# Output projection on two column groups of 256 outputs, in place of four of 128

## The chip, the cores and the metric

The kernel runs on one core of a Trainium2 chip. Of its engines, TensorE runs the matmuls and writes their sums into a memory called PSUM, VectorE and ScalarE copy results out of PSUM, and SyncE issues the transfers (DMA). A column group is a set of 32 of the columns of TensorE's array, which hold the 32 output rows here; groups can work side by side. The metric is the device time of one execution in microseconds (us), so lower is better. Profiles are of one execution; their span, from the first to the last instruction, is about 1.8 us shorter than the time.

## The reference

One decode step of attention with grouped heads: 32 sequences, one query row each, 32 query heads over 8 key/value heads of 128 values, a window of the last 512 of 2048 cached rows, and an output projection `wo` from 4096 to 512.

```
W = min(4096, max(256, Sk // 4))                    # 512
q = (x @ wq) as heads [32, 32, 1, 128]
k, v = the last W rows of k_cache, v_cache, each kv head repeated 4 times
scores = einsum("bhqd,bhkd->bhqk", q, k) * 128 ** -0.5
p = softmax(scores)
o = einsum("bhqk,bhkd->bhqd", p, v)
return o.reshape(32, 1, 4096) @ wo                  # the part that is changed
```

All inputs and the output are bfloat16. The output is 32 rows of 512 values.

## The kernel before

One queue (SyncE's) loads everything but the small input `x`: `wq`, then the blocks of K and V in a fixed order, then `wo` as eight head groups of 512 rows. The last group's load is cut in two: rows 0 to 2 of the four that each partition holds, and then row 3 alone. The kernel starts the output projection when the last V block has been used and the attention output has been brought into the order that it needs (`o_sel`). The parts that matter, with cuts marked:

```python
WO_CUT = 3
out_sb = x_sb.rearrange("b (c n) -> b c n", c=4)
# SyncE ...
for hg in range(NHG):                                      # 8 head groups
    for i0, i1 in ((0, 4),) if hg < NHG - 1 else ((0, WO_CUT), (WO_CUT, 4)):
        sp.dma_start(wo_sb[:, hg, i0:i1]..., wo[hg * 512:(hg + 1) * 512, :]...
        ).then_inc(sem_last if i0 else sem_wo[hg], 16)
sp.wait_ge(dve_out, 2)
sp.wait_ge(act_out, 2)
sp.dma_start(out..., out_sb...).then_inc(sem_out, 16)
# TensorE ...
for hg in range(NHG):
    pe.wait_ge(sem_wo[hg], 16)
    for i in range(4):
        if hg == NHG - 1 and i == WO_CUT:
            pe.wait_ge(sem_last, 16)
        for c in range(4):                                 # four column groups of the array
            ins = pe.matmul(
                X_ps[32 * c:32 * (c + 1), 2, 0:128],
                lhsT=o_sel[:, i, hg, :],
                rhs=wo_sb[:, hg, i, c * 128:(c + 1) * 128],
                start=(hg == 0 and i == 0), stop=(hg == NHG - 1 and i == 3),
                tile_position=(0, 32 * c),
            )
ins.then_inc(pe_fin, 1)
# VectorE, after pe_fin; ScalarE does the same with c = 2, 3
for c in range(2):
    dve.tensor_copy(out_sb[:, c, :], X_ps[32 * c:32 * (c + 1), 2, 0:128]).then_inc(dve_out, 1)
```

## Time and profile before

| | before |
|---|---|
| median time, 6 runs | 187.70 us (187.51 to 188.07) |
| span of the profiled execution | 185.9 us |
| the projection on TensorE | 128 matmuls, 178.72 to 183.27 us |
| start of the last head group to the end of the last copy | 182.71 to 183.91: 1.20 us |
| issue of the store | 183.98 us |

The prediction below shows the lines of the page and of the end of the timeline. Read them so: the DMA row says that the transfers fill the span, and the timeline says what still runs while the last of them land and after that. The row "start of the last head group to the end of the last copy" is the yardstick in the whole text: it does not depend on when the stream of transfers ends.

### The profile page before, as it was taken

To read this page: it belongs to the slowest core of one execution; us is meant where nothing else is said; L and a number is where in the kernel's file an instruction comes from. 1 tells how busy PE (TensorE), PEld (TensorE's weight loads), DVE (VectorE), ACT (ScalarE), POOL (GpSimd) and SP (SyncE) were. 2 spreads that over 40 slices of the span, in tenths; PEclk is the share of its full clock that TensorE was granted. 3 is DMA by queue.
4 is the path that set the end of the run, shared out by engine and by line. 5 is a ranking of instruction groups with operands and counts; after the bars stand their busy time and mean duration, and the time that the engine had idled before them with its cause. 6 is when DMAs were issued, how large, how long until landed. Compare 5 with 4: busy or idle time off the path is not lost.

```text
span 185.9 us, 3842 instructions
## 1 busy us (share of the span) xinstructions
PE 109.0 (59%) x1604; PEld 89.4 (48%) x1604; DVE 131.9 (71%) x239; ACT 82.3 (44%) x142; POOL 32.0 (17%) x82
## 2 busy tenths in 40 slices
PE   0232004336179906929906994159979975998752
PEld 0100001022069805819606974019949975987741
DVE  0006999689999999993699987999999995010001
ACT  3001000269320397020695018925998999910011
POOL 7100390500700080060240041000040000000000
PEclk9999999955557985885985599576999999999998
DMA  6999999999999999999999999999999999999980
GB/s 194 434 448 412 437 423 423 448 412 437 420 416 441 416 427 434 416 437 427 423 421 423 441 423 420 434 423 430 428 412 434 427 423 430 420 423 411 405 332 27
DMA packets 6304, 75.80 MB, mean 408 GB/s; under 512 B 720, under 2 KB 912, under 8 KB 1936
## 3 DMA queue, kind: packets, MB, share of 16 engines
q1 hardware_dynamic: 6240, 75.53, 96.4%
q8 instruction: 12, 0.20, 0.4%
q10 hardware_dynamic: 48, 0.03, 0.1%
q14 instruction: 4, 0.03, 0.0%
HBM read 75.53 MB, written 0.03 MB: 406 GB/s over the span
## 4 chain that ended last, share of the span: by engine, by line
DMA 64%; DVE 20%; PE 9%; issue 3%; SPq 3%; DVEq 0%
DMA V_sb<-in_v_cache_dram 31%; DMA K_sb<-in_k_cache_dram 14%; DMA w_sb<-in_wo_dram 12%; DVE KT_sb L431 12%; PE O_ps L356 8%; DMA w_sb<-in_wq_dram 6%; DVE w_sb L453 4%; DVE QA_sb L421 2%; SPq L214 2%; PE X_ps L299 1%; SPq L202 1%; DVE oT_sb L414 0%; DVE KT_sb L409 0%; PE X_ps L393 0%; DVE maxv L438 0%
## 5 line engine op out<-in xcount | busy, mean ns | idle before, releaser
L431 DVE STREAM_TRANSPOSE KT_sb<-K_sb 128x2048 uint32<-128x2048 uint32 x32 | 72.3, 2287 | 1.3 <-DMA K_sb<-in_k_cache_dram 1.1
L356 PE MATMUL O_ps<-w_sb,V_sb 128*128 128x128 bf16 x640 | 47.0, 244 | 9.6 <-DVE w_sb L453 5.0
L356 PEld LDWEIGHTS O_ps<-w_sb,V_sb 128*128 128x128 bf16 x640 | 45.6, 110 | 12.3 <-DVE w_sb L453 6.5
L268 POOL COPY QBD<-QA_sb 32x64 bf16<-32x64 bf16 x64 | 25.6, 540 | 81.2 <-PE S_ps L319 63.6
L520 ACT ACTIVATE w_sb<-PTc,mask 128x512 bf16<-128x512 bf16 x60 | 38.9, 729 | 0.0
L319 PE MATMUL S_ps<-KT_sb,QBD 128*32 128x512 bf16 x256 | 20.7, 475 | 26.6 <-DVE KT_sb L431 20.2
L453 DVE TENSOR_SCALAR w_sb<-PTc,mask 128x512 bf16<-128x512 bf16 x100 | 30.2, 370 | 6.3 <-PE O_ps L356 6.3
L319 PEld LDWEIGHTS S_ps<-KT_sb,QBD 128*32 128x32 bf16 x256 | 7.5, 110 | 36.5 <-issue 32.4
L492 ACT ACTIVATE X_ps<-S_ps,negmax 128x512 f32<-128x512 f32 x8 | 5.3, 657 | 42.8 <-DVE negmax L440 42.8
L338 PE MATMUL PT_ps<-P_bf,pick 128*128 128x128 bf16 x128 | 11.4, 260 | 17.9 <-ACT P_bf L501 14.7
L338 PEld LDWEIGHTS PT_ps<-P_bf,pick 128*128 128x128 bf16 x128 | 9.8, 119 | 20.9 <-ACT P_bf L501 16.3
L530 ACT ACTIVATE oT_sb<-O_ps 128x128 bf16<-128x128 f32 x8 | 6.0, 750 | 28.2 <-PE O_ps L356 28.2
L356 PE MATMUL O_ps<-K_sb,V_sb 128*128 128x128 bf16 x256 | 14.9, 217 | 3.5 <-DMA V_sb<-in_v_cache_dram 2.2
L356 PEld LDWEIGHTS O_ps<-K_sb,V_sb 128*128 128x128 bf16 x256 | 14.5, 96 | 4.3 <-issue 2.5
L520 ACT ACTIVATE K_sb<-PTc,mask 128x512 bf16<-128x512 bf16 x24 | 15.3, 725 | 1.6 <-DVE KT_sb L431 1.6
L453 DVE TENSOR_SCALAR K_sb<-PTc,mask 128x512 bf16<-128x512 bf16 x40 | 12.1, 377 | 0.3 <-ACT PTc L511 0.2
L474 DVE CAST K_sb<-S_ps 128x256 bf16<-128x256 f32 x1 | 0.4, 425 | 14.3 <-PE S_ps L368 14.3
L356 PE MATMUL O_ps<-KT_sb,V_sb 128*128 128x128 bf16 x128 | 7.5, 217 | 2.3 <-DMA V_sb<-in_v_cache_dram 2.3
L356 PEld LDWEIGHTS O_ps<-KT_sb,V_sb 128*128 128x128 bf16 x128 | 7.3, 96 | 2.5 <-issue 2.5
L520 ACT ACTIVATE KT_sb<-PTc,mask 128x512 bf16<-128x512 bf16 x12 | 7.7, 728 | 0.0
L501 ACT ACTIVATE P_bf<-X_ps,recip 128x512 bf16<-128x512 f32 x8 | 5.5, 684 | 4.5 <-DVE recip L446 4.4
L409 DVE CAST KT_sb<-X_ps 128x512 bf16<-128x512 f32 x1 | 0.7, 692 | 9.2 <-PE X_ps L299 9.2
(41 smaller groups left out, 49.6 us busy)
## 6 DMA issues: line engine op xcount, KB each, us to landing
K_sb<-in_k_cache_dram SPq DMA_DIRECT2D x16, 2048.0 KB, 15.1
V_sb<-in_v_cache_dram SPq DMA_DIRECT2D x16, 2048.0 KB, 16.8
w_sb<-in_wq_dram SPq DMA_DIRECT2D x2, 2048.0 KB, 9.7
w_sb<-in_wo_dram SPq DMA_DIRECT2D x7, 512.0 KB, 19.8
w_sb<-in_wo_dram SPq DMA_DIRECT2D x1, 384.0 KB, 22.6
w_sb<-in_wo_dram SPq DMA_DIRECT2D x1, 128.0 KB, 14.4
oT_sb<-in_x_dram ACTq DMA_DIRECT2D x1, 32.0 KB, 4.4
out_dram<-oT_sb SPq DMA_DIRECT2D x1, 32.0 KB, 1.5
```

Of the source, the lines that this page charges most:

```text
L214: sp.dma_start(wo_sb[:, hg, i0:i1].rearrange("p i n -> p (i n)"), wo[hg * 512:(hg + 1) * 512, :].rearrange("(m i) n -> m (i n)", i=4)[:, i ...
L268: pool.tensor_copy(dst[:, i, :, x0:x0 + 4], src).then_inc(pool_qbd, 1)
L319: ins = pe.matmul(S_ps[32 * c:32 * c + 32, q % 2, :], lhsT=QBD[:, q % 2, g, b, e, :], rhs=bass.AP(tensor=KT_sb, offset=s0 * slot + (b * G ...
L338: ins = pe.matmul(PT_ps[:, r, :], lhsT=pick[:, r, KS - s:KS - s + P], rhs=P_bf[:, s, :], start=(s == 0), stop=(s == KS - 1), tile_position ...
L356: ins = pe.matmul(O_ps[:, q % 2, 0:P], lhsT=V_sb[:, m % NV, r, :], rhs=z_of(q)[:, :, x0 + r, :], start=(e == 0 and r == 0), stop=(e == 1 a ...
L421: dve.tensor_copy(QA[32 * a:32 * a + 32, c], QW[32 * c:32 * c + 32, :, :, a::4].rearrange("p h k q -> p h q k"),).then_inc(dve_q, 1)
L431: dve.transpose(KT_w[:, n % NK, b].rearrange("p i r s -> p r i s"), K_w[:, n % NK, :, 32 * b:32 * b + 32],).then_inc(dve_T, 1)
L453: ins = dve.tensor_scalar(z_of(q)[:, k].rearrange("p x r -> p (x r)"), PTc[:, q % RING].rearrange("p x r -> p (x r)"), mask[:, k:k + 1], N ...
L492: act.activation(P_f32, S_ps[:, q % 2, :], ACTF.Exp, bias=negmax[:, q:q + 1], scale=SCALE, accum_out=sums[:, q:q + 1],).then_inc(act_exp, 1)
L501: act.activation(P_bf[:, :, :], P_f32.rearrange("p (x s) -> p s x", s=KS), ACTF.Copy, scale=recip[:, q:q + 1],).then_inc(act_P, 1)
L520: ins = act.activation(z_of(q)[:, k].rearrange("p x r -> p (x r)"), PTc[:, q % RING].rearrange("p x r -> p (x r)"), ACTF.Copy, scale=mask[ ...
L530: act.activation(oT_sb[:, :, 4 * q:4 * q + 4].rearrange("p h a -> p a h"), O_ps[:, q % 2, 0:P].rearrange("p (a h) -> p a h", a=4), ACTF.Co ...
```

## The change

Its intent is to have fewer and larger instructions at the end: half as many matmuls, and one copy for each engine in place of two. The words that came with it also name the load of one `wo` row for each partition at the end, which the diff does not touch. The diff, whole but for its line numbers and context:

```diff
-        out_sb = x_sb.rearrange("b (c n) -> b c n", c=4)
+        out_sb = x_sb.rearrange("b (c n) -> b c n", c=2)
...
-            sp.wait_ge(dve_out, 2)
-            sp.wait_ge(act_out, 2)
+            sp.wait_ge(dve_out, 1)
+            sp.wait_ge(act_out, 1)
...
-                    for c in range(4):
+                    for c in range(2):
                         ins = pe.matmul(
-                            X_ps[32 * c:32 * (c + 1), 2, 0:128],
+                            X_ps[32 * c:32 * (c + 1), 2, 0:256],
                             lhsT=o_sel[:, i, hg, :],
-                            rhs=wo_sb[:, hg, i, c * 128:(c + 1) * 128],
+                            rhs=wo_sb[:, hg, i, c * 256:(c + 1) * 256],
...
-            for c in range(2):
-                dve.tensor_copy(
-                    out_sb[:, c, :], X_ps[32 * c:32 * (c + 1), 2, 0:128]
-                ).then_inc(dve_out, 1)
+            dve.tensor_copy(out_sb[:, 0, :], X_ps[0:32, 2, 0:256]).then_inc(dve_out, 1)
...
-            for c in range(2, 4):
-                act.activation(
-                    out_sb[:, c, :], X_ps[32 * c:32 * (c + 1), 2, 0:128], ACTF.Copy
-                ).then_inc(act_out, 1)
+            act.activation(out_sb[:, 1, :], X_ps[32:64, 2, 0:256], ACTF.Copy).then_inc(act_out, 1)
```

## The prediction

> **What bounds the kernel now.** I read the page first, for the engine shares, the slices and the chain that ended last. The lines that carry it:
>
> ```profile
> PE 109.0 (59%) x1604; PEld 89.4 (48%) x1604; DVE 131.9 (71%) x239; ACT 82.3 (44%) x142; POOL 32.0 (17%) x82
> DMA  6999999999999999999999999999999999999980
> HBM read 75.53 MB, written 0.03 MB: 406 GB/s over the span
> DMA 64%; DVE 20%; PE 9%; issue 3%; SPq 3%; DVEq 0%
> ```
>
> No engine is near full, but the row of the 16 DMA engines is at 9 tenths from the second slice to the last but one. The kernel streams 75.53 MB, and the chain of waits is mostly transfers (64%). The change touches no transfer (the order of the SyncE instructions is the same in both kernels), so only the last slice and a half can move: what still runs once the stream is ending. For that I read the order of time of the last microseconds (start us, us, engine, line, operation, count, idle before it and what released it):
>
> ```profile
> 178.72 1.30 PE L393 MATMUL X_ps<-w_sb,K_sb 128*32 128x128 bf16 x80 [0.52 <-DVE K_sb L474]
> 180.52 0.41 PE L393 MATMUL X_ps<-w_sb,K_sb 128*32 128x128 bf16 x16 [0.50 <-DMA w_sb<-in_wo_dram]
> 181.75 0.41 PE L393 MATMUL X_ps<-w_sb,K_sb 128*32 128x128 bf16 x16 [0.82 <-DMA w_sb<-in_wo_dram]
> 182.71 0.56 PE L393 MATMUL X_ps<-w_sb,K_sb 128*32 128x128 bf16 x16 [0.55 <-DMA w_sb<-in_wo_dram]
> 183.32 0.56 ACT L547 ACTIVATE oT_sb<-X_ps 32x128 bf16<-32x128 f32 x2 [5.81 <-PE X_ps L393]
> 183.32 0.59 DVE L477 CAST oT_sb<-X_ps 32x128 bf16<-32x128 f32 x2 [4.66 <-PE X_ps L393]
> 183.98 0.36 SPq L220 DMA_DIRECT2D out_dram<-oT_sb  x1
> ```
>
> These are the output projection: eight head groups of 16 matmuls, one per wo block. The first five blocks are there when it starts at 178.72; groups 5, 6 and 7 each wait for their block, so by then TensorE follows the DMA. Cut more finely, the last 16 split in two: 12 start by 182.9, the other four at 183.03, which is where the separate last 128 KB load (issued about 168.5, 14.4 us to landing, so about 182.9) lets them go. They end at 183.27, two copies run on VectorE beside two on ScalarE, and the last copy ends at 183.32 + 0.59 = 183.91. Then the store is issued at 183.98 and the span ends at 185.9. **The path of the tail:** landing of the last wo row, last matmuls, evacuation, store.
>
> The words of the change name a last load of one wo row for each partition. The kernel before has that load already (its cut is at row 3 of 4) and the diff does not touch it. I give it no gain.
>
> **What the Trainium skill says.** (1) "TensorE: Matmul & The Clock Gate", section "Single matmul latency": a warm matmul of N columns takes (398+N)/2.4 ns. For N = 128 that is 219 ns; this trace has 219 as the median of the projection's 128 matmuls, and a granted clock of 1.00 from 176 to 184 us, so it agrees. The same formula gives 272.5 ns for N = 256. (2) "TensorEngine Tiling (Array Packing)", section "Tiling Modes": with 128 rows and 32 columns there are four tiles, which work independently. The trace agrees: 80 matmuls in 1.30 us are (1.30 - 0.219)/79 = 13.7 ns from start to start, a quarter of the 53.3 ns that 128 columns take at 2.4 GHz. (3) "ScalarE: Activation LUTs", section "What ACT_TABLE_LOAD costs": an activation with immediate scale and bias takes 186 ns + 0.833 ns per element, which is 293, 506 and 612 ns at 128, 384 and 512; the trace has 270, 490 and 597, so the slope agrees and the constant is some 20 ns lower here. (4) "DMA: Bandwidth & Descriptors", section "Where the ~2 µs actually goes": most of a small transfer's fixed time is the receipt of the write. The store of 32 KB took 1.5 us from issue to landing here, and its size and shape in memory stay, so I leave it alone.
>
> **The change part by part.**
>
> Matmuls: 128 of 128 columns on four column groups become 64 of 256 columns on two. The streamed columns stay 16,384, but half as many groups take them at once. A pair of 256 columns occupies its groups for 256/2.4 = 107 ns, so the whole projection needs 32 x 107 = 3.4 us of streaming in place of 128 x 13.7 = 1.75 us. Fewer instructions is therefore more TensorE time. Where does it lie?
> - Groups 0 to 4: 20 rounds, the last of which starts at 178.72 + 19 x 0.107 = 180.75 and ends at 181.02, in place of 180.02.
> - Group 5's block was there at 180.52 at the latest, so it follows at once: four rounds, 180.86 to 181.18, ending near 181.45 in place of 180.93.
> - Group 6's block comes at 181.75. The array has been free since about 181.3, so the lag is gone with 0.4 us to spare. It runs to 181.75 + 3 x 0.107 + 0.27 = 182.34.
> - Group 7 starts at 182.71 as before. Three rounds for its first three rows start at 182.71, 182.82 and 182.92; the array is free for the fourth at 183.03, which is just when the last load releases it. So the last pair starts at 183.03 as before, or a few tens of ns later, and ends one longer latency on: + (272.5 - 219) = +0.05 us. Before, the last of four starts some ten ns after the first; that is now one pair. Net **+0.04 us** on the path.
>
> Evacuation: two copies of 32x128 on each engine become one of 32x256. VectorE from PSUM in this trace: 280 ns for 128 elements per partition, 425 for 256 (the 128x256 copy of the last selection), 556 for 384, 692 for 512, or about 1.06 ns per element on 145 fixed. I take 0.42 us for 32x256, since the time follows the elements per partition. It was 0.59 with the gap between the two: -0.17. ScalarE: 270 for 128, 490 for 384, so about 0.38 for 256 in place of 0.56: -0.18. VectorE remains the later one, so **-0.17 us** on the path.
>
> Store, waits and the rest: the SyncE waits count 1 instead of 2 on each engine; no cost. The 32 rows of 1 KB in the output tile are the same bytes. 64 matmuls and 64 weight loads fewer are less to fetch, but TensorE does not bound the place where they are. **0.**
>
> Sum: +0.04 - 0.17 = -0.13 us. In the trace's terms the last copy ends at 183.32 + 0.04 + 0.42 = 183.78 and not 183.91, so the time becomes 187.71 - 0.13 = 187.58, which I call **187.6 us**.
>
> **The rivals.**
>
> TensorE becomes the bound of the tail. If the two groups did not overlap (64 x 107 = 6.8 us), or if the clock were granted at half (32 rounds of 213 ns, the same 6.8 us), the projection would end at 178.72 + 6.8 + 0.2 = 185.7 rather than 183.27, so the time would be some 2.4 us longer, 190.0 us (+1.3%), still within 2%. Against it: the four groups overlap fully before, and the clock reads 1.00 throughout that stretch. The change keeps TensorE busier there, so the clock should not fall. I give this 4%.
>
> A smaller form: only the last block sees it. If group 7's first six matmuls are not through when the last row lands (a landing earlier than 183.03 with the same landing of the 384 KB), the fourth round waits for the third and up to 0.1 us of the copy's gain is given back: 187.65 to 187.7. The spare is nil by my working, so I give that one chance in three.
>
> The evacuation's gain is hidden. It would be if the store waited for something else. But the page of the DMA queue's own waits shows the store waiting 13.4 us with ScalarE's copies named as the releaser, and it is issued 0.07 us after the last copy. There is no other wait between. Yet 0.13 us is 0.07% of the time, and the three runs before lie between 187.68 and 188.07, so the gain can drown in the jitter of a stream of 75 MB: 187.7 to 187.9 measured, with the mechanism right.
>
> The stream itself changes. It would take another order of transfers or another time at which a buffer comes free; the first 178 us of every engine's program are the same in both kernels, so I see no path to it.
>
> **Range and chances.** 187.58 is the centre of the sum. Below, I allow 0.3 us: the gain is at most the whole 0.17 of the copies plus jitter of the stream. Above, 0.4: the before-runs reach 0.36 above their median. So 187.3 to 188.0 should hold it 8 times in 10. A change of 2% would be 3.75 us. The whole of the tail after the last landing is about 3 us and the worst case of TensorE is +2.4, so neither side is within reach by this mechanism: faster 0.01, same 0.98, slower 0.01.
>
> **What would show it right or wrong.** In the profile of the changed kernel the projection should be 64 matmuls of about 272 ns, the first 40 lasting about 2.3 us instead of 1.30; group 6 and 7 should still be released by a wo transfer; the last pair should end within 0.1 us of the old distance from the last landing; one copy of about 0.42 us on VectorE and 0.38 us on ScalarE should stand before the store, which should again follow within 0.1 us; and the span should be near 185.8. It is wrong if TensorE is still busy with an earlier group when group 6's or 7's block lands (no idle ahead of the group), if the 32x256 copy costs as much as the two did, or if the transfers land at other times than before for a reason outside the change.

## More of the kernel before

The 32 output rows of a column group land on their own 32 partitions of PSUM, so the four groups' results lie on four sets of 32 partitions, and the copies bring them side by side onto the partitions 0 to 31 for the store.

## The result

The changed kernel took 187.60 us (median of 6 runs, 187.29 to 188.04) against 187.70 us of the kernel before. The ratio is 0.9992 with a 95% interval of 0.9976 to 1.0007: the same within noise. Ratios here are worked out from the fast runs of both kernels, and not quite the ratio of the medians quoted.

The page of the changed kernel, same rows as in the prediction:

```profile
PE 109.5 (59%) x1540; PEld 90.0 (48%) x1540; DVE 131.5 (71%) x238; ACT 82.3 (44%) x141; POOL 32.0 (17%) x82
DMA  6999999999999999999999999999999999999980
HBM read 75.53 MB, written 0.03 MB: 407 GB/s over the span
DMA 56%; DVE 26%; PE 11%; issue 4%; SPq 3%; DVEq 0%
```

There are 64 matmuls fewer (1604 to 1540) and yet TensorE is busy a little longer. The DMA row is the same digit for digit. The shares of the chain differ in its earlier part, in which none of the changed lines stands; why was not followed up. The end of the timeline of the changed kernel (start us, us, engine, line, operation, count, idle before and its releaser):

```profile
178.67 2.80 PE L393 MATMUL X_ps<-w_sb,K_sb 128*32 128x256 bf16 x48 [0.52 <-DVE K_sb L474]
181.83 0.61 PE L393 MATMUL X_ps<-w_sb,K_sb 128*32 128x256 bf16 x8 [0.36 <-DMA w_sb<-in_wo_dram]
182.80 0.61 PE L393 MATMUL X_ps<-w_sb,K_sb 128*32 128x256 bf16 x8 [0.35 <-DMA w_sb<-in_wo_dram]
183.45 0.37 ACT L543 ACTIVATE oT_sb<-X_ps 32x256 bf16<-32x256 f32 x1 [6.00 <-PE X_ps L393]
183.45 0.41 DVE L476 CAST oT_sb<-X_ps 32x256 bf16<-32x256 f32 x1 [4.84 <-PE X_ps L393]
183.92 0.36 SPq L220 DMA_DIRECT2D out_dram<-oT_sb  x1
```

Groups 0 to 5 now run in one piece of 48 matmuls and 2.80 us. Groups 6 and 7 still wait for the transfer, with 0.36 and 0.35 us of idle ahead of them. The last group takes 0.61 us where it took 0.56, and the later copy 0.41 where the two took 0.59. From the start of the last group to the end of the last copy it is 183.45 + 0.41 - 182.80 = 1.06 us, 0.14 below the 1.20 of before. The span is only 0.1 us shorter, as the last group was let go 0.09 us later in this execution than in that of before (182.80 against 182.71).

| | before | changed |
|---|---|---|
| projection's matmuls, median ns each | 219 | 273 |
| last head group on TensorE, us | 0.56 | 0.61 |
| later copy or copies (VectorE), us | 0.59 | 0.41 |
| start of last group to last copy's end, us | 1.20 | 1.06 |
| time, us | 187.70 | 187.60 |

### The profile page after: what moved, and what is told of

It is laid out like the page before. It is cut to its first block, busy times and chain, and to the rows that moved or that the text cites. A ratio compares the mean times of both kernels' runs of the same rounds, so it can differ in the third digit from the quotient of the medians.

```text
span 185.8 us, 3712 instructions
## 1 busy us (share of the span) xinstructions
PE 109.5 (59%) x1540; PEld 90.0 (48%) x1540; DVE 131.5 (71%) x238; ACT 82.3 (44%) x141; POOL 32.0 (17%) x82
## 4 chain that ended last, share of the span: by engine, by line
DMA 56%; DVE 26%; PE 11%; issue 4%; SPq 3%; DVEq 0%
DMA V_sb<-in_v_cache_dram 31%; DVE KT_sb L431 16%; DMA w_sb<-in_wo_dram 12%; PE O_ps L356 7%; DMA w_sb<-in_wq_dram 7%; DMA K_sb<-in_k_cache_dram 6%; DVE w_sb L453 6%; DVE QA_sb L421 2%; PE S_ps L319 2%; SPq L214 2%; PE X_ps L299 1%; DVE maxv L438 1%; SPq L202 1%; DVE oT_sb L414 0%; DVE KT_sb L409 0%
## 5 line engine op out<-in xcount | busy, mean ns | idle before, releaser
L356 PE MATMUL O_ps<-w_sb,V_sb 128*128 128x128 bf16 x640 | 45.9, 241 | 11.1 <-DMA V_sb<-in_v_cache_dram 6.1
L356 PEld LDWEIGHTS O_ps<-w_sb,V_sb 128*128 128x128 bf16 x640 | 44.5, 108 | 13.8 <-issue 7.5
```

The source lines that it names most:

```text
L356: ins = pe.matmul(O_ps[:, q % 2, 0:P], lhsT=V_sb[:, m % NV, r, :], rhs=z_of(q)[:, :, x0 + r, :], start=(e == 0 and r == 0), stop=(e == 1 a ...
```

## The experiments

My theory was the sum of the prediction: a longer last pair of matmuls gives +0.05 us, one copy for two gives -0.17. The rivals: nothing on the path has changed; TensorE becomes the bound; a part of the gain comes from elsewhere. One run of this kernel scatters by several tenths of a microsecond, more than the effect. So most verdicts rest on distances within a trace, and one experiment repeats the step to lift it out of the noise. All the kernels gave the reference's output.

### The changed kernel again, twice

No edit.

> The changed kernel itself, for more rounds. My theory (a longer last pair of matmuls, +0.05 us, and one copy in place of two, -0.17 us): about 0.13 us below the kernel before, 187.6 against 187.7, ratio 0.9993. Rival (nothing on the path changed, the difference is jitter of the stream): ratio 1.0000. The jitter of one run is about 0.2 us, so I expect the interval to be hardly narrow enough; the distance in the profile from the start of the last head group to the end of the last copy should be 1.06 us again (1.20 before).

The four fast runs of five gave a ratio of 0.9993 (0.998 to 1.0007). The profiled execution took 288.79 us, with TensorE's work stretched throughout (the projection's 64 matmuls took 9.59 us, on average 527 ns each, although the clock for it is 1.00). Nothing is read from it, and why it was slow is open. So the kernel was run again beside a later experiment:

> The changed kernel once more beside the three-piece run, because its last profile fell in a disturbed execution: 187.6 us, ratio to before 0.9993, and 1.06 us from the start of the last head group to the end of the last copy.

The ratio was 0.9992 (0.9976 to 1.0008), with medians of 187.75 and 187.77 us. Three comparisons thus lie at 0.9992, 0.9993 and 0.9992, where 0.9993 was expected, but each interval contains 1; the measured times alone do not show the gain. The profiled execution was one of the longer ones (188.38 us), and just this makes it useful:

```profile
179.95 3.33 PE L393 MATMUL X_ps<-w_sb,K_sb 128*32 128x256 bf16 x56 [0.52 <-DVE K_sb L474]
183.64 0.61 PE L393 MATMUL X_ps<-w_sb,K_sb 128*32 128x256 bf16 x8 [0.36 <-DMA w_sb<-in_wo_dram]
184.29 0.41 DVE L476 CAST oT_sb<-X_ps 32x256 bf16<-32x256 f32 x1 [4.39 <-PE X_ps L393]
```

The last group and its copy come 0.84 us later than in the first profile of this kernel, and the distance is again 184.29 + 0.41 - 183.64 = 1.06 us. The scatter lies ahead of the tail, and the tail can be measured apart from it. Other traces repeat the distance too: 1.06 and 1.07 us for the changed kernel in the runs with repeated steps and with measured copies below, and 1.21 for the kernel before in its run with repeated steps (183.72 + 0.59 - 183.10). One thing differs here: the projection started 1.28 us later (179.95 against 178.67), and groups 0 to 6 ran in one piece of 56 matmuls with no idle of TensorE ahead of group 6. That comes close to a sign that the prediction gave for being wrong. It cost nothing, since group 7 still waited 0.36 us for its transfer, but it shows how little room two groups leave.

### The new matmuls with the old number of copies

```diff
-            dve.tensor_copy(out_sb[:, 0, :], X_ps[0:32, 2, 0:256]).then_inc(dve_out, 1)
+            for h in range(2):
+                dve.tensor_copy(
+                    out_sb[:, 0, h * 128:(h + 1) * 128], X_ps[0:32, 2, h * 128:(h + 1) * 128]
+                ).then_inc(dve_out, 1)
```

and the same on ScalarE, with the waits back at 2.

> The changed matmuls alone (two column groups of 256), with each engine's copy cut in two of 128 columns again. My theory: the copies cost 0.59 us on VectorE as before and the last pair of matmuls is 0.05 us longer, so start of the last head group to end of the last copy is 1.25 us and the time 0.05 us above the kernel before. Rival (what helped was the smaller number of matmuls and weight loads): the distance stays near 1.06 us.

Ratio 0.9993 (0.998 to 1.0007), median 187.41 us; the timing tells nothing apart. In the trace:

```profile
182.61 0.61 PE L393 MATMUL X_ps<-w_sb,K_sb 128*32 128x256 bf16 x8 [0.35 <-DMA w_sb<-in_wo_dram]
183.26 0.48 DVE L477 CAST oT_sb<-X_ps 32x128 bf16<-32x128 f32 x2 [4.71 <-PE X_ps L393]
```

The matmul part is as expected, 0.61. The copies are not: two of 128 columns took 0.48 us together, not the 0.59 of the kernel before, and the distance is 183.26 + 0.48 - 182.61 = 1.13 us, between the two expectations. The copies have the same shape and number as before; what differs is that both now read the same 32 partitions of PSUM, and not two sets of 32. So of the 0.18 us that the copies gave, only 0.07 (0.48 to 0.41) is for having one instruction in place of two, and 0.11 (0.59 to 0.48) for something that I had not named. The next run looks for it.

### Copies measured by themselves

Behind the changed kernel's own copies, five rows of eight copies on VectorE and then the same five on ScalarE, each into columns of its own. The VectorE rows in short:

```python
for j in range(8):   # row 1: same source and destination partitions
    ins = dve.tensor_copy(probe(0, j), S_ps[0:32, 1, cols(j)])
# row 2: source S_ps[32 * (j % 2):32 * (j % 2) + 32, ...], destination partitions 0 to 31
# row 3: source and destination both in turn;  row 4: only the destination in turn
# row 5: 128 partitions, always the same
```

> The changed kernel with a measuring block behind its two copies: on VectorE, then on ScalarE, five rows of eight copies of 128 columns from one bank of PSUM: from and to the same 32 partitions; from two sets of 32 partitions in turn to one set; both in turn; only the destination in turn; and 128 partitions. Theory A (a copy overlaps the one before it only if both read the same partitions): eight take 0.28 + 7 x 0.20 = 1.7 us on VectorE with one source and 8 x 0.31 = 2.5 us with the source in turn, whatever the destination. Theory B (the destination decides): the row with only the destination in turn takes 2.5 us and that with only the source in turn 1.7. Theory C (neither; the two-copies run differed by chance of issue): all rows alike.

```profile
183.93 1.66 DVE L485 CAST KT_sb<-S_ps 32x128 bf16<-32x128 f32 x8
185.52 2.45 DVE L488 CAST KT_sb<-S_ps 32x128 bf16<-32x128 f32 x8
188.00 2.47 DVE L491 CAST KT_sb<-S_ps 32x128 bf16<-32x128 f32 x8
190.50 2.45 DVE L494 CAST KT_sb<-S_ps 32x128 bf16<-32x128 f32 x8
192.98 1.67 DVE L497 CAST KT_sb<-S_ps 128x128 bf16<-128x128 f32 x8
194.69 1.38 ACT L568 ACTIVATE KT_sb<-S_ps 32x128 bf16<-32x128 f32 x8 [10.80 <-DVE KT_sb L497]
195.97 2.31 ACT L571 ACTIVATE KT_sb<-S_ps 32x128 bf16<-32x128 f32 x8
```

The rows that stay on the same partitions (the first and the last of VectorE) take 1.66 us; every row with a partition set in turn, whether of the source, of both or of the destination, takes 2.45 or more. The spacing is (1.66 - 0.27)/7 = 0.20 us in the first and (2.45 - 0.28)/7 = 0.31 in the others, each copy being 0.27 to 0.28 us long. So theories A and B were each half right and C fell: a copy overlaps the end of the one before it only if both read from and write to the same set of partitions. ScalarE does the same: 0.16 us apart on the same partitions, 0.29 in turn (its other two rows in turn, not shown, also took 2.31 us). The two pairs of copies come out of these spacings: 0.20 + 0.28 = 0.48 us on one set, 0.31 + 0.28 = 0.59 on two. The Trainium skill has this for VectorE ("VectorE: DVE Perf Modes", section "Two Vector instructions with no wait between them"): an instruction is held until all earlier ones have finished if an input or its output starts in another group of 32 partitions than the last read from, or write to, the same memory. This trace agrees: 0.31 us apart where the group changes, 0.20 where it stays. I had not used it. This was one look, a single run, so its state is unknown; the reading rests on spacings within that trace.

### One column group of 512

```diff
-                    for c in range(2):
+                    for c in range(1):
-                            X_ps[32 * c:32 * (c + 1), 2, 0:256],
+                            X_ps[32 * c:32 * (c + 1), 2, 0:512],
-                            rhs=wo_sb[:, hg, i, c * 256:(c + 1) * 256],
+                            rhs=wo_sb[:, hg, i, :],
```

with one copy of 32x512 on VectorE and none on ScalarE.

> One column group of 512 columns, so 32 matmuls, and one copy of 32x512 on VectorE. My theory (streaming time per head group is columns over groups at work): 32 x 213 ns = 6.8 us of TensorE from the start of the projection, so it ends near 178.7 + 6.8 + 0.2 = 185.7 and the copy takes 0.69 us: about 2.5 us longer than before, 190.2 us, and no idle ahead of head groups 6 and 7. Rival (few large matmuls are cheap however many groups they use, as the tail waits for transfers anyway): within 0.4 us of before.

190.02 us (median of 4 runs), ratio 1.0126 (1.0112 to 1.014): +2.4 us, where +2.5 was expected.

```profile
178.62 7.08 PE L392 MATMUL X_ps<-w_sb,K_sb 128*32 128x512 bf16 x32 [0.52 <-DVE K_sb L473]
185.74 0.68 DVE L475 CAST oT_sb<-X_ps 32x512 bf16<-32x512 f32 x1 [7.17 <-PE X_ps L392]
```

All 32 matmuls stand in one unbroken piece of 7.08 us, with no idle ahead of groups 6 and 7: TensorE is now the bound of the tail. The working was that the time of the columns is divided by the number of groups at work, so 6.8 us of streaming with one. This run confirms it at the far end (31 rounds of 0.213 us and one matmul of 0.379 are 6.98), and that two groups are the fewest that fit under the transfers here. It is the rival "TensorE becomes the bound" of the prediction, with its 190.0 us, one step further along the same road.

### Four groups and one copy over 128 partitions

```diff
-            for c in range(2):
-                dve.tensor_copy(
-                    out_sb[:, c, :], X_ps[32 * c:32 * (c + 1), 2, 0:128]
-                ).then_inc(dve_out, 1)
+            dve.tensor_copy(out_sb, X_ps[:, 2, 0:128]).then_inc(dve_out, 1)
-                out.rearrange("b s n -> b (s n)"), out_sb[:, :, :].rearrange("b c n -> b (c n)")
+                out.rearrange("b s (c n) -> c (b s) n", c=4), out_sb
```

against the kernel before; ScalarE copies nothing, and `out_sb` is a tile of 128 partitions by 128.

> The four column groups of 128 as before, but one copy of 128 partitions x 128 columns on VectorE in place of four copies of 32x128, and the store from 128 partitions with rows of 256 bytes. My theory (a copy costs by elements per partition, not by partitions): the copy takes 0.28 us, start of the last head group to end of the copy 0.56 + 0.05 + 0.28 = 0.89 us, 0.31 below before and 0.17 below the changed kernel, so 187.4 us if the store still takes 1.5 us. Rival (the short rows of the store take it back): store over 1.8 us and no gain.

187.99 us, ratio 1.0015 (1.0002 to 1.0027): a little slower than before, though far within the 2% that count as the same.

```profile
182.57 0.56 PE L392 MATMUL X_ps<-w_sb,K_sb 128*32 128x128 bf16 x16 [0.55 <-DMA w_sb<-in_wo_dram]
183.19 0.29 DVE L475 CAST oT_sb<-X_ps 128x128 bf16<-128x128 f32 x1 [4.62 <-PE X_ps L392]
183.51 0.69 SPq L219 DMA_DIRECT2D out_dram<-oT_sb  x1
```

The copy did what the theory says, 0.29 us for four times the partitions, and the distance is 183.19 + 0.29 - 182.57 = 0.91 us. But the store takes it all back: its issue takes 0.69 us where it took 0.36, and the final wait for its landing is 1.5 us where it was 1.1. That is 0.7 us lost for 0.29 gained. What the rival expected came about, but not that the short rows are its cause. The Trainium skill ("DMA: Bandwidth & Descriptors", section "Specifications") gives 512 bytes as the least transfer at full rate; the rows here have 256. The packets in the packed traces agree that short ones cost more for each byte (18 ns for 256 bytes, 47 for 1 KB), but they show something else as well. The store before ends with 16 completion packets of 4 bytes, and its data packets run for 0.29 us; the store here ends with only four, as many as the first dimension of its new order has entries, and its data packets run for 0.53 us. It looks as if fewer of the 16 DMA engines took part; spread over all of them, 128 packets of 18 ns would be 0.14 us (an estimate). So the order of dimensions is a rival to the shortness and the number of the rows, and no run separates them.

### The last step, repeated twenty times

Both kernels got a chain behind the projection: the last step's matmuls into another bank, then the copies into a scratch tile, and TensorE waits for both copies before the next step. For the changed form:

```python
for t in range(20):
    pe.wait_ge(dve_out, t + 1); pe.wait_ge(act_out, t + 1)
    for c in range(2):
        ins = pe.matmul(O_ps[32 * c:32 * (c + 1), 0, 0:256], lhsT=o_sel[:, 3, NHG - 1, :],
                        rhs=wo_sb[:, NHG - 1, 3, c * 256:(c + 1) * 256], start=True, stop=True, tile_position=(0, 32 * c))
    ins.then_inc(pe_fin, 1)          # VectorE and ScalarE: one copy of 32x256 each, into scratch
```

and for the old form four matmuls of 128 and two copies on each engine.

> The kernel before with its last step repeated 20 times at the end in a chain: four matmuls of 128 columns on four groups, then two copies of 32x128 on each of two engines into a scratch tile, and TensorE waits for both before the next. The step's own cost, as I work it out: 0.23 of matmuls, 0.05 to the copies, 0.59 of copies, 0.05 and more back, about 0.95 us, so some 19 us over the kernel before.

> The changed kernel with its last step repeated 20 times in the same chain: two matmuls of 256 columns, one copy of 32x256 on each engine. My theory (+0.05 us of matmul latency, -0.18 us of copies for each step): 20 x 0.13 = 2.6 us below the run with the old step repeated (between 2.2 and 3.0 allowed). Rival (the step's cost does not depend on the form): within 0.4 us of it.

208.81 us with the old form and 206.60 with the new: 2.21 us between them, far outside the scatter (208.63 to 209.31 and 206.45 to 206.65), at the lower edge of what I allowed. The old form lies 21.1 us above the kernel before in the same call (187.73), where some 19 were expected. The old form's trace, with the row of a later stretch (start to end, us, then each engine's busy time, the granted clock, DMA share and rate):

```profile
184.42 0.24 PE L407 MATMUL O_ps<-w_sb,K_sb 128*32 128x128 bf16 x4 [0.76 <-DVE oT_sb L490]
200.45 0.30 PE L407 MATMUL O_ps<-w_sb,K_sb 128*32 128x128 bf16 x4 [0.76 <-DVE P_bf L496]
195.00:205.00 10.00, 2.98 (x40) 1.40 (x40) 5.11 (x19) 4.90 (x19) 0.00 (x0) 0.50 0.00 0
```

And the new form's:

```profile
184.16 0.29 PE L407 MATMUL O_ps<-w_sb,K_sb 128*32 128x256 bf16 x2 [0.56 <-DVE oT_sb L489]
200.14 0.40 PE L407 MATMUL O_ps<-w_sb,K_sb 128*32 128x256 bf16 x2 [0.56 <-DVE P_bf L492]
195.00:202.90 7.90, 3.18 (x16) 1.07 (x16) 3.56 (x9) 3.23 (x9) 0.00 (x0) 0.50 0.00 0
```

TensorE is busy for only 2.98 of 10.00 us in such a stretch of the old form, and the clock granted in both forms is 0.50. At this clock the new form's longer matmuls weigh more: 0.40 against 0.30 us, and not 0.29 against 0.24 as at the full clock. From one step's first matmul to the next it is 1.00 and 0.84 us at the full clock (0.16 saved) and 1.05 and 0.95 at the half one (0.10 saved). Taking 0.14 for the real last step, two repeated steps at 0.16 and 18 at 0.10 gives 2.3 us for the measured 2.21. This leaves out that one step of the old form, during which the clock fell, took 1.33 us in this profile, the slowest of the four runs. I had given each step 0.13; I had not reckoned with the half clock, and whether the chain itself brought it about is not shown.

### The last load in one piece, and in three

The changed kernel without the cut of the last `wo` block:

```diff
-                for i0, i1 in ((0, 4),) if hg < NHG - 1 else ((0, WO_CUT), (WO_CUT, 4)):
+                for i0, i1 in ((0, 4),):
```

with TensorE's wait for the last row taken out, since the one load's semaphore now covers it.

> The changed kernel with the last wo block loaded in one transfer of 512 KB. My theory: its landing falls where that of the last 128 KB did, about 0.2 to 0.3 us after the landing of the 384 KB, and then all eight matmuls run, 0.60 us rather than 0.28: up to 0.3 us longer than the changed kernel, at most. If the cut does nothing (its landing is not later than that of the 384 KB): the same as the changed kernel within 0.1 us, and the last pair in the changed kernel waited for its slot on the array only.

```profile
181.81 0.62 PE L391 MATMUL X_ps<-w_sb,K_sb 128*32 128x256 bf16 x8 [0.23 <-DMA w_sb<-in_wo_dram]
183.05 0.61 PE L391 MATMUL X_ps<-w_sb,K_sb 128*32 128x256 bf16 x8 [0.62 <-DMA w_sb<-in_wo_dram]
```

The last group starts 1.24 us after group 6, in place of 0.97 with the cut (0.95 to 0.98 in the five traces that have it): 0.27 us later, and everything behind it too. The medians (187.73 us, and 187.73 for the kernel before in the same call, ratio 0.9996 with 0.9976 to 1.0016) are too coarse for it. So the cut is worth 0.27 us on the path by these distances, but the kernel before has it as well. The 0.61 us here is without any wait inside the group. It equals the 0.61 with the cut, so in the changed kernel the last row's landing costs nothing on top of the array's own time. The last group of the kernel before took 0.56 where groups 5 and 6 took 0.41: there it does cost 0.15.

With three loads of two rows, one and one:

```diff
-                for i0, i1 in ((0, 4),) if hg < NHG - 1 else ((0, WO_CUT), (WO_CUT, 4)):
+                for i0, i1 in ((0, 4),) if hg < NHG - 1 else ((0, 2), (2, 3), (3, 4)):
```

with one more semaphore for the middle piece.

> The changed kernel with the last wo block in three loads of 2, 1 and 1 rows. My theory (the last pair of matmuls waits for its place on the array behind six others, and not for the last row): the first rows land earlier, the array is free when the last row lands, and the last pair starts some 0.08 us earlier with respect to head group 6: 0.08 us faster than the changed kernel. Rival (the last row's landing lets the pair go, or another load costs as much): no gain or a loss of up to 0.2 us.

187.68 us, ratio to before 1.0001 (0.9982 to 1.0019): no gain. The weight loads of TensorE tell when each piece let it go:

```profile
182.31 0.11 PEld L396 LDWEIGHTS X_ps<-w_sb,K_sb 128*32 128x32 bf16 x4 [0.33 <-DMA w_sb<-in_wo_dram]
182.65 0.10 PEld L396 LDWEIGHTS X_ps<-w_sb,K_sb 128*32 128x32 bf16 x2 [0.23 <-DMA w_sb<-in_wo_dram]
182.98 0.10 PEld L396 LDWEIGHTS X_ps<-w_sb,K_sb 128*32 128x32 bf16 x2 [0.23 <-DMA w_sb<-in_wo_dram]
```

The pieces of 128 KB come 0.34 and 0.33 us apart, about what 128 KB take at the 407 GB/s of the stream (0.32 us). Group 6 started at 181.66, so the last pair is let go 1.32 us behind it; in the changed kernel the last pair starts 1.31 behind (the group ends at 183.41, a matmul is 0.273 long). My expectation fell: the array is free earlier, but the last row does not land earlier, and the pair waits for that instead. So, as far as these spacings tell, both conditions come due within hundredths of a microsecond of each other in the changed kernel, and little is left to gain on either alone.

No version tried beats the changed kernel beyond the noise.

## Why the prediction was right

**The sum.** -0.13 us was forecast, 187.58 us. The tail became 0.14 us shorter by the trace, and the median is 0.10 lower; as that is well inside the scatter, it is partly luck that it falls so near the forecast. The range of 187.3 to 188.0 held the median, and the class "same" was the one given 0.98.

**The matmuls, +0.04.** Measured +0.05 (0.56 to 0.61). Each step of it is to be seen: 273 ns for one matmul of 256 (272.5 worked out), no idle between groups 0 to 5, idle ahead of groups 6 and 7 (ahead of 7 alone in the late execution), and an array that is free for the last pair when the last row lands. The piece of 48 matmuls in 2.80 us is 23 rounds of 0.107 us and one matmul's length, 2.73 by that working. The "smaller form" among the rivals, given one chance in three, did not come about: the run without the cut shows 0.61 with all rows there, the same.

**The copies, -0.17.** Measured -0.18 on VectorE (0.59 to 0.41) and -0.19 on ScalarE (0.56 to 0.37). The size was right, but the reason given with it was only half the story. I took each copy as a fixed part and a part by columns, so that merging two saves a fixed part. The run with two copies shows that merging in itself is worth 0.07. The larger 0.11 came from the new layout: each engine stays on one set of 32 partitions, where before its second copy read another set and could not overlap the first. Taking 0.59 from the trace of before had hidden this error from the sum.

**The store and the stream, 0.** The store's issue (0.36 us) and landing (1.5) did not change. The scatter of the whole time lies ahead of the tail, as a profile that ran 0.84 us late with the same tail of 1.06 shows.

**The rivals.** TensorE as the bound is real but one halving away: it cost +1.3% with one group. (In the late execution the idle ahead of group 6 was gone already.) "The gain drowns in the jitter" is what the measured times showed; only the repeated step lifted it out.

## What to carry to other kernels

When transfers fill the span, first find what is still to be done behind the last landing; a change to other work gains nothing unless it moves the stream, and this part can be measured to hundredths within a trace though the whole time scatters by tenths. Fewer matmuls are not less TensorE time: with column groups, time is columns divided by groups at work, so count rounds before merging. And lay out results so that an engine's consecutive copies stay on one set of 32 partitions, and look at what the store becomes, the length of its rows and the order of its dimensions, before you spread a tile over more of them.

## What the Trainium skill lacked or had wrong

- "ScalarE: Activation LUTs" (section "What ACT_TABLE_LOAD costs") says that back-to-back activations overlap by about 93 ns. The runs agree on the same partitions (0.26 us long, 0.16 apart), but the page lacks that there is no overlap when the set of 32 partitions changes (0.27 us long, 0.29 apart). For VectorE the skill has the rule, on its own page.
- "DMA: Bandwidth & Descriptors" calls the time to generate descriptors small and variable, in its section on the gpsimd path ("Anatomy of one DMA — SWDGE (gpsimd) path"). It has no figure for how the issue of a transfer from SyncE depends on its shape: a 32 KB store took 0.36 us to issue with 32 rows of 1 KB and 0.69 with 128 rows of 256 bytes in another order of dimensions, both on the path at a kernel's end.
